# A gated recurrence and two gated feed-forward layers on one core: a step's loads one piece earlier in another order, its output gate a piece later, and one fold moved to where its result is read

## The chip, the cores and the metric

One core of a Trainium2 chip runs the whole program in one launch. The metric is the device time of that core in microseconds (us), lower is better. Three runs of the kernel before gave 875.76, 877.87 and 878.70 us, the median is 877.87 us.

## What is computed

The input is a recurrence over 768 time steps (4 sequences, 8 heads of 40 channels, the matrix state kept as `C`), and then two gated layers over the 3,072 tokens of 320 channels. Cut to what matters:

```python
for t in range(S):                                   # 768 steps
    m_new = np.maximum(f_gate[:, :, t] + m, i_gate[:, :, t])
    f_stab = np.exp(f_gate[:, :, t] + m - m_new)
    i_stab = np.exp(i_gate[:, :, t] - m_new)
    C = f_stab * C + i_stab * outer(vt, kt);  n = f_stab * n + i_stab * kt
    y[:, :, t] = sigmoid(o_gate[:, :, t]) * (C @ qt) / maximum(abs(n @ qt), 1)
x = (sigmoid(x @ w_gate) * (x @ w_val)) @ w_out      # d_ff 1536
h = x @ w_in;  out = (h * clip(h + 3, 0, 6) / 6) @ w_out   # d_ff 2048
```

## The kernel before, in words

The recurrence is done in 6 chunks of 128 time steps. One chunk of one sequence, (c, b), is called a step below, and is made in three pieces. Piece 0 (`att0`, L412) computes the scores on TensorE (L363), turns the decay rows of the step into a decay matrix by two scans on VectorE (L389), scales the values (L354, L383) and weighs the scores by the decays (L404). In the kernel before it also applies the sigmoid to the output gate, in place, on ScalarE (L410). Piece 1 (`att1`, L429) makes the outputs on TensorE: the part of the carried state (L445), the part inside the chunk (L456), and the state's increment (L471, not in the last chunk); then the denominators (L488 to L497), the product with the gate (L505) and the new state (L523, L526, L531). Piece 2 (`att2`, L533) transposes the result on TensorE (L537) and splits it into a rounded and a remaining part (L542 on ScalarE, L543 on VectorE). The pieces of a chunk run in the order 0.0, 0.1, 1.0, 0.2, 1.1, 2.0, 1.2, 2.1, 3.0, 2.2, 3.1, 3.2 (sequence.piece).

A step works on three tiles that are loaded from memory: `qk` (512 KB, L212), `vko` (values, keys, output gate; 480 KB, L215) and `dec` (the decay rows, one row read by all 128 partitions; 512 KB, L223). Each has two buffers, so the loads of step b + 2 go into the buffers of step b: `qk` is free after L445 of that step, `dec` after L456, and `vko` after L505.

The matrix multiplications of the first gated layer run between the pieces: in the main loop (L864) each pass over one block of 128 hidden channels takes at most two pieces, then the two products of the block (`m1_h`, L576; L555 to L562), then the output products of an earlier block (`m1_out`, L586; L597, L607), then, in every second pass from chunk 2 on, one job (`work`, L662) that fetches a block of raw second-layer weights (L94), converts it (L119, L122), combines it (L638 to L641) and stores it (L645, L646, L622). One of these stores, L646, writes runs of 128 bytes. Chunk c of the layer runs beside the recurrence of chunk c + 1, so in the last chunk of the layer there is none. At the end of a chunk `m1_end` (L609) copies the three accumulators out of PSUM. The third one holds two halves of 64 partitions that have to be added; the kernel before does that there: two half copies (L616, L617) and an addition (L618), then it stores the chunk to `x2_dram` (L619). The second layer (from L970) reads the chunks back in pairs (`x_load`, L793, at L801 and L803) and multiplies by a scheme of seven products (L914), with `m2_out` (L951 to L953) behind them.

PSUM has 8 banks: 3 for `mm`, 3 for `acc`, 2 for `att`. The scores of a step take both `att` banks until L404 has read them, its outputs take both until L491, its transposes one until L543.

All loads and stores are issued by one queue, that of SyncE (SP). Order is set in two ways. The text of the program gives the order within an engine among things that are ready, and a planner that knows only estimated durations may put an instruction ahead of earlier ones when it reckons its operands to be there; on the chip each engine then works through its queue in that fixed order, so that an instruction whose operand is late holds up all behind it. A block under `issue_after(ins)` puts its instructions behind `ins` on the engine of `ins`.

The head of the key product that reads past its own columns matters below: in L467 and L473 the columns of `vko` from the keys on are read in runs of 32, and the last run (head 7, second run) takes columns 312 to 343 of a 320-column key block, so it takes 24 columns of the output gate with it.

Of the kernel before, what the change touches and what calls it, by code (L numbers as in the profile page):

```python
# [8 lines left out]
F32 = mybir.dt.float32  # L9
# [11 lines left out]
NC = S // L  # L21
# [11 lines left out]
def mlstm_then_two_gated_ffn(  # L33
# [183 lines left out]
    def att_load(c, b):  # L217
        att_tiles(c, b)
        qk_load(c, b)
        vko_load(c, b)  # L220

    def dec_load(c, b):
        nc.sync.dma_start(  # L223
            out=at[c, b]["dec"].rearrange("p h l -> p (h l)"),
            in_=fz_dram[c, b * H : (b + 1) * H, :]
            .rearrange("h l -> (h l)")
            .rearrange("(o n) -> o n", o=1)
            .to_broadcast([P, H * L]),
        )
# [178 lines left out]
    def out_gate(c, b):  # L408
        o = at[c, b]["vko"][:, 2, :]
        nc.scalar.activation(out=o, in_=o, func=AF.Sigmoid)  # L410

    def att0(c, b, ps):  # L412
        scores(c, b, ps)
        if c == 1:
            values(c, b, True)
        value_ones(c, b)
        for n in range(2):
            decays(c, b, n)
        if c != 1:
            values(c, b, False)  # L420
        if c < NC - 1:
            values_end(c, b, c == 0)
        for n in range(2):
            weigh(c, b, n)

        with tc.issue_after(last_exp[-1]):
            out_gate(c, b)

    def att1(c, b, ps):  # L429

        outputs(c, b, ps)
        y = denominators(c, b)
        gated(c, b, y, c == 1 and b < 2)
        state(c, b)
# [141 lines left out]
    def m1_h(c, f, ts):  # L576
        n = ts.stop - ts.start
        banks = [ps_mm()[:, :n], ps_mm()[:, :n]]
        h_pair(slots["in", f], (1, c), banks, ts)
        g = gpool.tile([P, T], F32, tag="g", name="g")[:, :n]  # L580
        gate = nc.scalar.activation(out=g, in_=banks[0], func=AF.Sigmoid).ins  # L581
        nc.vector.tensor_tensor(out=g, in0=g, in1=banks[1], op=ALU.mult)  # L582
        gs[c, f, ts.start] = split_g(g)
        return gate
# [24 lines left out]
    def m1_end(c):  # L609
        a = acc1.pop(c)  # L610
        x2 = xpool.tile([P, 3, T], F32, tag="x2", name="x2")
        for m in range(2):
            nc.scalar.copy(out=x2[:, m, :], in_=a[m])

        sw = gpool.tile([P, T], F32, tag="g", name="sw")
        nc.scalar.copy(out=sw[0:64], in_=a[2][64:128])  # L616
        nc.scalar.copy(out=sw[64:128], in_=a[2][0:64])  # L617
        nc.vector.tensor_tensor(out=x2[:, 2, :], in0=sw, in1=a[2], op=ALU.add)  # L618
        nc.sync.dma_start(out=x2_dram[c], in_=x2)  # L619

    def store_w2(n, x):
# [171 lines left out]
    def x_load(pair):  # L793


        b = {}
        for k in range(2):
            for j in range(2):
                src = x2_dram[2 * pair + j]
                t = b[k, j] = late.tile([P, 640], F32, tag="c", name="xr", bufs=7)  # L800
                nc.sync.dma_start(out=t[:, 0:T], in_=src[:, k, :])  # L801
                for q in range(4):
                    nc.sync.dma_start(  # L803
                        out=t[32 * q : 32 * q + 32, T:],
                        in_=src[32 * k : 32 * k + 32, 2, q * P : (q + 1) * P],
                    )
        return x_combine(pair, b)

    def x_combine(pair, b):
# [54 lines left out]
    for i, (c, f, ts) in enumerate(steps):  # L864
        if i == halves[0] - 1:
            for b in range(2):
                att_load(1, b)
                dec_load(1, b)
        for _ in range(quota[i]):
            if pieces:  # L870
                cp, b, piece = pieces.pop(0)
                if cp > 0 and b == 0 and piece == 0:
                    x_tiles((1, cp))
                with ExitStack() as queued:
                    for ins in opened if cp == 0 else ():
                        queued.enter_context(tc.issue_after(ins))
                    (att0, att1, att2)[piece](cp, b, ps_att)
                nxt = divmod(cp * B + b + 2, B)
                if cp > 0 and piece == 2 and nxt[0] < NC:
                    att_load(*nxt)  # L880
                    dec_load(*nxt)
        gate = m1_h(c, f, ts)
        outputs_but(2 if i < n_two else 1)
        before.append((c, f, ts))
        if c == 0:
            work(1 if i < 2 * halves[0] else 2, n_w1)
        elif c < NC - 1:

            with tc.issue_after(gate):
                work(c > 1 and f % 2 == 0, n_jobs)  # L890
        elif f == 0:
            assert not jobs and not pieces
            early_sb.close()
            late = ctx.enter_context(tc.tile_pool(name="late", bufs=1, reuse_waits="tile"))
            x_parts = x_load(0)
            load_group(0)
        else:
            if f > 1 and f - 2 < F2 // 2:
                load_out2(f - 2)
            next(x_parts, None)  # L900
# [187 lines left out]
```

## Time and profile before

| what | value |
|---|---|
| median of three runs | 877.87 us |
| the profiled execution's own time | 880.01 us |
| its span, first to last instruction | 878.2 us |
| mean granted TensorE clock | 0.992 |
| TensorE matmul busy | 838.4 us (95%) |
| VectorE busy | 568.0 us (65%) |
| ScalarE busy | 399.3 us (45%) |
| share of the 16 DMA engines, queue of the loads and stores | 47.2% |

The span is 1.8 us shorter than the time of the same execution, which has its start and end around it. The profiled execution took 2.1 us more than the median. Granted clock means the share of full speed (2.4 GHz) that TensorE got. An engine that is idle costs time only when TensorE, which is busy nearly all the time, has to wait for it.

### The profile page before, as it was taken

What the parts mean: (1) busy time and instruction counts of PE and PEld (TensorE: products, weight loads), DVE (VectorE), ACT (ScalarE), POOL (GpSimd) and SP (SyncE); (2) the same over time, 40 slices, a digit from 0 to 9 for tenths busy, and PEclk for the clock granted to TensorE, in tenths of its full rate; (3) what the DMA queues carried; (4) which work ended last, traced back from release to release, by engine and by line L of the source; (5) the groups of instructions that cost most, each with busy time, mean ns of one, the idle gap of its engine ahead of it and who ended that gap; (6) DMA issues with size and microseconds to landing.
All of it is one profiled execution on the core that took longest, in us unless ns stands there. A gap on an engine that the chain in (4) does not pass through costs nothing.

```text
span 878.2 us, 17340 instructions
## 1 busy us (share of the span) xinstructions
PE 838.4 (95%) x7109; PEld 715.0 (81%) x7109; DVE 568.0 (65%) x1034; ACT 399.3 (45%) x813; POOL 2.5 (0%) x8
## 2 busy tenths in 40 slices
PE   6599899999999899989999999999999999999998
PEld 6488679887777777777778888888898888988898
DVE  7899965766587668655845553666746567466553
ACT  3687733332343234323322543556545555455542
POOL 1000000000000000000000000000000000000000
PEclk9999999999999999989999999999999999999999
DMA  9636723422655465456433632556734566344400
GB/s 356 224 116 214 253 72 108 143 72 72 200 202 177 156 200 203 156 176 198 142 85 94 178 85 73 181 163 185 235 99 147 153 197 220 109 151 146 146 31 31
DMA packets 67599, 134.86 MB, mean 154 GB/s; under 512 B 20672, under 2 KB 41600, under 8 KB 64448
## 3 DMA queue, kind: packets, MB, share of 16 engines
q1 hardware_dynamic: 67472, 133.65, 47.2%
q8 instruction: 56, 0.92, 0.5%
q14 instruction: 23, 0.19, 0.1%
q10 hardware_dynamic: 48, 0.10, 0.0%
HBM read 108.59 MB, written 25.13 MB: 152 GB/s over the span
## 4 chain that ended last, share of the span: by engine, by line
PE 80%; DVE 9%; DMA 8%; issue 2%; ACT 1%; SPq 0%; DVEq 0%; ACTq 0%
PE mm L914 9%; PE acc L597 9%; DMA dec<-fz_dram 7%; PE mm L561 6%; PE mm L560 6%; PE mm L559 6%; PE acc L914 4%; PE att L914 4%; PE mm L555 4%; PE mm L562 3%; PE acc L607 3%; DVE dec L389 3%; PE mm L951 2%; PE mm L953 2%; PE mm L952 2%; PE att L363 2%
## 5 line engine op out<-in xcount | busy, mean ns | idle before, releaser
L568 ACT CAST gh<-g 128x512 fp32r<-128x512 f32 (+1 forms) x130 | 76.1, 588 | 131.1 <-DVE g L582 109.0
L559 PE MATMUL mm<-x,w 128*128 128x512 f32 (+1 forms) x328 | 122.2, 373 | 0.0
L560 PE MATMUL mm<-x,w 128*128 128x512 f32 (+1 forms) x328 | 122.1, 372 | 0.0
L561 PE MATMUL mm<-x,w 128*128 128x512 f32 (+1 forms) x328 | 122.1, 372 | 0.0
L569 DVE TENSOR_TENSOR gl<-g,gh 128x512 fp32r<-128x512 f32 (+1 forms) x130 | 84.0, 648 | 55.9 <-ACT gh L568 55.1
L597 PE MATMUL acc<-gh,w 128*128 128x512 f32 (+1 forms) x328 | 104.2, 363 | 0.0
L914 PE MATMUL mm<-X,wg 128*128 128x512 f32 x336 | 85.5, 395 | 1.0 <-DMA wg<-wt_dram 1.0
L582 DVE TENSOR_TENSOR g<-g,mm 128x512 f32<-128x512 f32 (+1 forms) x82 | 50.6, 617 | 43.3 <-PE mm L562 43.2
L914 PEld LDWEIGHTS mm<-X,wg 128*128 128x128 f32 x336 | 61.9, 188 | 14.4 <-DMA wg<-wt_dram 1.2
L560 PEld LDWEIGHTS mm<-x,w 128*128 128x128 f32 x328 | 63.3, 193 | 11.1
L389 DVE TENSOR_TENSOR_SCAN dec<-dec,ident 128x512 f32<-128x512 f32 x40 | 48.0, 1217 | 37.5 <-DMA dec<-fz_dram 37.5
L561 PEld LDWEIGHTS mm<-x,w 128*128 128x128 f32 x328 | 63.1, 193 | 11.2
L559 PEld LDWEIGHTS mm<-x,w 128*128 128x128 f32 x328 | 63.6, 194 | 8.9
L555 PE MATMUL mm<-x,w 128*128 128x512 f32 (+1 forms) x164 | 68.0, 414 | 2.6 <-DVE cst L526 1.6
L581 ACT ACTIVATE g<-mm 128x512 f32<-128x512 f32 (+1 forms) x82 | 44.6, 544 | 54.3 <-PE mm L562 54.0
L597 PEld LDWEIGHTS acc<-gh,w 128*128 128x128 f32 x328 | 60.3, 188 | 10.5
L562 PE MATMUL mm<-x,w 128*128 128x512 f32 (+1 forms) x164 | 60.4, 368 | 0.0
L597 PE MATMUL acc<-gl,w 128*128 128x512 f32 (+1 forms) x164 | 59.9, 365 | 0.0
L929 ACT ACTIVATE gb<-c,half 128x512 f32<-128x512 f32 x48 | 34.3, 723 | 44.6 <-DVE c L925 44.5
L569 DVE TENSOR_TENSOR gl<-gb,gh 128x512 fp32r<-128x512 f32 x48 | 33.0, 691 | 30.6 <-ACT gh L568 30.6
L914 PE MATMUL att<-X,wg 128*128 128x512 f32 x168 | 46.9, 397 | 0.0
L568 ACT CAST gh<-gb 128x512 fp32r<-128x512 f32 x48 | 29.5, 620 | 37.1 <-PE att L952 37.1
(187 smaller groups left out, 1695.5 us busy)
## 6 DMA issues: line engine op xcount, KB each, us to landing
wg<-ws_dram SPq DMA_DIRECT2D x24, 1104.0 KB, 5.5
raw<-in_w SPq DMA_DIRECT2D x20, 640.0 KB, 4.0
qk<-in_qkT SPq DMA_DIRECT2D x22, 512.0 KB, 5.1
wg<-wt_dram SPq DMA_DIRECT2D x48, 224.0 KB, 6.3
vko<-in_vko SPq DMA_DIRECT2D x22, 480.0 KB
dec<-fz_dram SPq DMA_DIRECT2D x20, 512.0 KB, 5.0
raw<-in_wo SPq DMA_DIRECT2D x14, 640.0 KB, 3.8
X<-xt_dram SPq DMA_DIRECT2D x84, 64.0 KB, 3.1
```

The source lines that it names most:

```text
L389: nc.vector.tensor_tensor_scan(out=x, data0=a["factors"][n] if "factors" in a else x, data1=ident4.rearrange("p h l -> p (h l)"), initial= ...
L555: nc.tensor.matmul(out=banks[j], lhsT=tail, rhs=xl[:, 2, :], start=True, stop=False)
L559: nc.tensor.matmul(out=banks[j], lhsT=hi, rhs=xh[:, k, :], start=False, stop=False)
L560: nc.tensor.matmul(out=banks[j], lhsT=hi, rhs=xl[:, k, :], start=False, stop=False)
L561: nc.tensor.matmul(out=banks[j], lhsT=lo, rhs=xh[:, k, :], start=False, stop=False)
L562: nc.tensor.matmul(out=banks[j], lhsT=tail, rhs=xh[:, 2, :], start=False, stop=True)
L568: nc.scalar.copy(out=gh, in_=g)
L569: nc.vector.tensor_tensor(out=gl, in0=g, in1=gh.bitcast(F32), op=ALU.subtract)
L581: gate = nc.scalar.activation(out=g, in_=banks[0], func=AF.Sigmoid).ins
L582: nc.vector.tensor_tensor(out=g, in0=g, in1=banks[1], op=ALU.mult)
L597: nc.tensor.matmul(out=a[m], lhsT=lhsT, rhs=rhs, start=st and lhsT is hi and rhs is gh, stop=en and lhsT is lo, skip_group_check=True,)
L914: nc.tensor.matmul(out=ps, lhsT=w[a][s], rhs=x[:, b, :], start=first and i == 0, stop=i == 3, skip_group_check=True,)
```

## The change

There are three edits. The loads of the step after the next are written after piece 1 of a step, where they were written after piece 2, and in the order `dec`, `qk`, `vko` in place of `qk`, `vko`, `dec`. The sigmoid of the output gate is written in piece 1 behind the output matmuls, where it was at the end of piece 0. The two halves of the third accumulator are stored as they are, and are added when the second layer reads them: each of the four tail loads of a tile fetches both halves (32 KB, was 16 KB) into a new tile `xu`, and an addition of 128x128 elements on VectorE writes the tail. `xu` has the tag `xt`, whose three buffers the splits in `x_combine` use too.

```diff
+    def att1(c, b, ps):
+
+        outputs(c, b, ps)
         with tc.issue_after(last_exp[-1]):
             out_gate(c, b)
-
-    def att1(c, b, ps):
-
-        outputs(c, b, ps)
         y = denominators(c, b)
@@ def m1_end(c):
-        for m in range(2):
+        for m in range(3):
             nc.scalar.copy(out=x2[:, m, :], in_=a[m])
-
-        sw = gpool.tile([P, T], F32, tag="g", name="sw")
-        nc.scalar.copy(out=sw[0:64], in_=a[2][64:128])
-        nc.scalar.copy(out=sw[64:128], in_=a[2][0:64])
-        nc.vector.tensor_tensor(out=x2[:, 2, :], in0=sw, in1=a[2], op=ALU.add)
         nc.sync.dma_start(out=x2_dram[c], in_=x2)
@@ def x_load(pair):
                 nc.sync.dma_start(out=t[:, 0:T], in_=src[:, k, :])
+                u = late.tile([P, 2, P], F32, tag="xt", name="xu", bufs=3)
+                tails = src[:, 2, :].rearrange("(two k r) (q t) -> k q r two t", two=2, k=2, q=4)[k]
                 for q in range(4):
-                    nc.sync.dma_start(
-                        out=t[32 * q : 32 * q + 32, T:],
-                        in_=src[32 * k : 32 * k + 32, 2, q * P : (q + 1) * P],
-                    )
+                    nc.sync.dma_start(out=u[32 * q : 32 * q + 32], in_=tails[q])
+                nc.vector.tensor_tensor(out=t[:, T:], in0=u[:, 0], in1=u[:, 1], op=ALU.add)
@@ main loop
-                if cp > 0 and piece == 2 and nxt[0] < NC:
-                    att_load(*nxt)
+                if cp > 0 and piece == 1 and nxt[0] < NC:
+                    att_tiles(*nxt)
                     dec_load(*nxt)
+                    qk_load(*nxt)
+                    vko_load(*nxt)
```

## Rows read from the trace of the kernel before

**Rows 1.** Windows of core 0: stretch, then length and busy us of PE, PEld, DVE, ACT, POOL; clock, DMA.

```profile
100.00:460.00 360.00, 345.70 (x3766) 281.90 (x3766) 240.33 (x467) 125.73 (x272) 0.00 (x0) 0.98 0.46 150
...
540.00:878.00 338.00, 330.82 (x1840) 297.16 (x1838) 198.66 (x314) 178.74 (x308) 0.00 (x0) 1.00 0.47 147
```

**Rows 2.** Timeline of PE: start us, us, instruction, [idle before it <- releaser].

```profile
130.22 0.44 PE L537 MATMUL att<-ident,yo 128*128 128x128 f32 x2 [0.67 <-DVE dec L404]
...
244.11 0.38 PE L456 MATMUL att<-vi,dec 128*32 128x41 f32 x18 [1.97 <-DVE x L543]
...
300.01 0.38 PE L363 MATMUL att<-qk 40*128 40x128 f32 x2 [2.38 <-DVE x L543]
...
331.51 0.44 PE L456 MATMUL att<-vi,dec 128*32 128x41 f32 x16 [2.24 <-DVE x L543]
...
389.30 0.38 PE L363 MATMUL att<-qk 40*128 40x128 f32 x2 [2.45 <-DVE x L543]
...
421.56 0.32 PE L456 MATMUL att<-vi,dec 128*32 128x41 f32 x12 [1.50 <-DVE x L543]
```

**Rows 3.** Windows at a lower clock, columns as in Rows 1.

```profile
300.92:304.33 3.41, 3.41 (x11) 2.54 (x9) 2.46 (x4) 0.62 (x1) 0.00 (x0) 0.50 0.02 5
331.64:335.05 3.41, 3.41 (x100) 3.01 (x97) 2.55 (x8) 1.16 (x4) 0.00 (x0) 0.50 0.96 339
389.67:396.49 6.82, 6.82 (x27) 5.44 (x24) 2.76 (x5) 1.91 (x3) 0.00 (x0) 0.50 0.00 0
```

**Rows 4.** Waits between 100 and 460 us: engine, line, releaser: total us, times, longest us.

```profile
ACT vko L410 <- DMA vko<-in_vko: 56.3, 13, 6.7
DVE dec L389 <- DMA dec<-fz_dram: 37.5, 13, 5.7
...
DVE vi L354 <- DMA vko<-in_vko: 10.3, 3, 4.5
```

**Rows 5.** Timeline of DVE around 240 and 297 us, columns as in Rows 2.

```profile
238.08 2.34 DVE L389 TENSOR_TENSOR_SCAN dec<-dec,ident 128x512 f32<-128x512 f32 x2 [5.67 <-DMA dec<-fz_dram]
...
243.51 0.55 DVE L543 TENSOR_TENSOR x<-att,x 128x384 fp32r<-128x384 f32 x1
...
297.17 2.34 DVE L389 TENSOR_TENSOR_SCAN dec<-dec,ident 128x512 f32<-128x512 f32 x2 [4.20 <-DMA dec<-fz_dram]
```

**Rows 6.** Timeline of SP's queue: start us, us of the issue, line, transfer.

```profile
226.18 0.56 SPq L646 DMA_DIRECT2D wt_dram<-bits  x1
226.84 3.75 SPq L212 DMA_DIRECT2D qk<-in_qkT  x1
230.70 0.37 SPq L215 DMA_DIRECT2D vko<-in_vko  x1
231.12 0.42 SPq L223 DMA_DIRECT2D dec<-fz_dram  x1
...
288.37 3.15 SPq L212 DMA_DIRECT2D qk<-in_qkT  x1
291.62 0.38 SPq L223 DMA_DIRECT2D dec<-fz_dram  x1
```

**Rows 7.** Line L223: the landing of the decay rows after their issue.

```profile
DMA to landing us min/median/max: 4.9/5.0/5.6
```

**Rows 8.** Timeline of ACT around 298 us, columns as in Rows 2.

```profile
298.50 0.47 ACT L410 ACTIVATE vko<-vko 128x320 f32<-128x320 f32 x1 [6.26 <-DMA vko<-in_vko]
298.88 0.46 ACT L542 CAST x<-att 128x384 fp32r<-128x384 f32 x1
```

**Rows 9.** Lines L618, L819: duration ns min/median/max; then the landing of L803's loads.

```profile
L618 DVE TENSOR_TENSOR x<-sw,acc x6: 679/686/687, 140.0 to 548.8; 128x512 f32<-128x512 f32 x6
...
L819 DVE TENSOR_TENSOR xt<-xr,xt x21: 280/285/291, 473.7 to 754.7; 128x128 fp32r<-128x128 f32 x21
...
DMA to landing us min/median/max: 1.8/2.8/6.1
```

**Rows 10.** Timeline of PE at the end of a pair's first half.

```profile
623.48 0.41 PE L951 MATMUL acc<-w,gh 128*128 128x320 f32 x1 [1.33 <-ACT gh L568]
```

## The prediction, written before the change was run

> **What bounds the kernel now.** I first read the busy shares on the page and then the windows. TensorE is the bound: between 100 and 460 us, where the recurrence runs beside the first layer, it is busy for 345.70 of 360 us, so it idles for 14.3 us, and from 540 us on, in the second layer, it idles for 7.2 of 338 us [rows 1]. The stretch up to 460 us is the one that the moved loads touch. The timeline of PE then shows what ended its idle times there: six of them hold 11.2 of the 14.3 us, one ended by VectorE's weighing of scores (L404), five by its splitting of a transposed result (L543), which sets a bank of the two `att` banks free [rows 2]. So PE waits for VectorE, not for a load. Windows laid over the granted clock add a second price: after the gaps of 2.38, 2.24 and 2.45 us TensorE ran at 1.2 GHz in place of 2.4 for 3.41, 3.41 and 6.82 us; after those of 1.97 and 1.50 us it did not [rows 2, 3]. At half the clock half of these 13.6 us is lost, 6.8 us. All that this stretch can give back is therefore 14.3 + 6.8 = 21.1 us, 2.4%.
>
> Next I read why VectorE is late. The view of the waits names two transfers: the scans waited 37.5 us for `dec`, 13 times; ScalarE's sigmoid waited 56.3 us for `vko`, 13 times, and the values another 10.3 us for it [rows 4]. The scan at 238.08 us sits in VectorE's queue 5.67 us before its rows are there, and L543 at 243.51 us, for which PE waits, stands behind it [rows 5]. In the same way the sigmoid holds up ScalarE: at 298.50 us it had waited 6.26 us, and the first half of the split (L542), without which L543 can't start, came right behind it [rows 8].
>
> Last, SP's queue shows why `dec` is late: the transfer that follows a store of short runs (L646) takes 3.75 us to issue, `vko` comes next, and `dec` is issued at 231.12 us and usable at 238.08, 6.96 us later, where decay rows with less ahead of them need 5.0 [rows 5, 6, 7].
>
> **The change part by part.** *Order and place of the loads.* Each of the three issues stays, with its bytes; none is added. SP already takes the loads as soon as the buffers are free, ahead of text that comes earlier: they stand right behind L646, which belongs to a job of an earlier pass and keeps its place before them [rows 6]. So I cost the earlier place by itself at nothing, with bounds of 0 and, where a fetch or store is passed, one issue of 0.4 us [rows 6], 16 times, 6.4 us at most. `vko` keeps its wait for L505 and holds up on SP what is behind it, a fetch or a chunk's store, as it does now; `dec` has to wait for L456 a little after L445, and `qk` behind it that much longer, but `qk` is wanted a full step later. The order is worth more. At 226.84 us `dec` would take the slow place: its issue ends at 230.59 and began at 230.2 at the latest, it lands 5.0 us later at 235.2, 2.9 us earlier than 238.08 [rows 5, 6, 7]. At 288.37 us only `qk` stood before it: the issue would count from 291.1, landing at 296.1 for 297.17, 1.1 us earlier [rows 5, 6, 7].
>
> The rule that I weigh against this row is that of the Trainium skill, page "DMA: Bandwidth & Descriptors", section "Anatomy of one DMA — SWDGE (gpsimd) path": about 2.0 us fixed and the bytes at 436 GB/s, an estimate of 3.2 us for 512 KB, fitted on another queue path than SP's. The trace has 5.0 us, never under 4.9 [rows 7], and decides; by the page every load would land 1.8 us sooner still, the gaps at 300.01 and 331.51 us would close, and the sum below would be 2.9 us more, 867.4 us.
>
> Gap by gap [rows 2]: 244.11, 1.97 us, closes, since 2.9 us is more than that: 1.97. 300.01: two scans of 2.34 us behind 296.1 end at 298.4, L543 comes at 298.4 for 299.4 if ScalarE is out of the way (next part): 1.0, which leaves 1.4. 331.51: there the values wait for `vko` too, which now comes last, so I take 0.7, which leaves 1.5. 421.56: the same in the last chunk, 0.3. 389.30: nothing, see below. 130.22: `dec` was issued when it could be, only `qk` goes out of its way, 0.5 of 0.67. The rest of the idle time, 3.1 us in pieces under these, 0.3. Sum 4.8 us, bounds 0 (if the scans move up as much as the rows do) and 14.3. The clock: 1.4 and 1.5 us are nearest to the gaps after which it stayed, so two stretches of 3.41 us go, 2 x 1.7 = 3.4 us; bounds 0 and 6.8 [rows 3].
>
> *The sigmoid.* By text it only moves; but the increment (L471) reads 24 columns of the gate with the keys, so behind it the sigmoid has to wait for L471 where before L471 waited for the sigmoid. That takes it off the landing of `vko` and puts it in the 3 us or so in which VectorE makes the denominators; 0.47 us [rows 8] on ScalarE is covered by them, and if they did not cover it, it would cost 0.47 per step. In the last chunk there is no L471: nothing ties the sigmoid, it may stay at the landing of `vko`, and so I leave 389.30 and its 6.82 us at half clock as they are [rows 2, 3]. Its worth is in the 1.0 and 0.7 above.
>
> *The fold.* Six times ScalarE is rid of a copy and VectorE of 0.69 us [rows 9]; none of PE's large idle times is ended there [rows 2], so nothing, bounds 0 and 0.69 each. In its place come 12 additions of 128x128, 4 before each pair; the nearest row is L819 with 0.285 us [rows 9]. The first four run in the long last chunk of the first layer. The others stand in the second layer, where VectorE is busy 59% [rows 1]; at the end of a pair's first half PE waits 1.33 us for a chain through VectorE and ScalarE [rows 10], and I let one addition fall into it: 0.3, twice, 0.6 us. Bounds: nothing, and a full landing before it, below.
>
> Sum: 4.8 + 3.4 - 0.6 = 7.6 us. The profiled execution took 880.01 us and would take 872.4; it was 2.1 us over the median of 877.87, so for the median I say **870.3 us**.
>
> **The rivals.** *All gaps close.* If rows land before the planner's place for the scans everywhere, 21.1 - 0.6 = 20.5 us go: 857.4 us. For it speaks that one reason is named for 104 us of waits [rows 4]; against it that near 130 us and 389 us the load has nothing to pass.
>
> *The scans move along.* The planner placed the scans where it reckoned the rows to be there. If it reckons them earlier, it puts scans and values further up, VectorE stands still just as long, and L543 stays behind it; the gain is 0 and the fold's 0.6 us remains: 878.5 us, no change. The place of the scan at 238.08, far ahead of its use, speaks for it [rows 5]; against it, that the delay at SP comes from a slow issue of 3.75 us [rows 6], of which a planner with estimated durations need not know.
>
> *The additions stall the second layer.* They are queued on VectorE and wait for a load that lands after 2.8 us, in one case 6.1 [rows 9]. If one landing stands ahead of the chain that PE waits for, the gap of 1.33 us [rows 10] grows by 2.8 + 0.3 = 3.1 us, which brings it to more than all gaps after which the clock fell, and 1.7 to 3.4 us are lost with that [rows 2, 3]: 4.8 to 6.5 us in each of two pairs, 9.6 to 13.0, in the middle 11.3. Against the 8.2 us gained before the fold this is 3.1 us slower, 881.0 us. It decides from 4.1 us a pair on. Against it: VectorE idles 41% there [rows 1], and the loads come a group ahead of that gap.
>
> **How the numbers follow.** The forecast has a chance of 0.48, its own range is 864 to 876. All gaps close 0.14, scans move along 0.20, additions stall 0.18. A measurement of this kernel can tell 0.3% from no change, that is 2.6 us, from 875.2 to 880.5. Forecast and closing together give 0.62 faster, the moving scans 0.20 the same, the stall 0.18 slower. The range reaches from 857.4 to the middle of the stall, 881.0; outside are half of the stall and the outer edges.
>
> **What would show it.** Right: scans around 238 and 297 us wait under 3.5 and 3.2 us, L410 waits for L471 in chunks 2 to 4 and for `vko` in the last alone, windows around 300 and 331 us at full clock, PE idles about 9.5 us between 100 and 460 us. Wrong: `dec` still issued behind another load after L646; the waits at L389 still near 37 us; gaps at L951 over 2 us; new idle times between 540 us and the end.

## The result and the profile after

The changed kernel took 881.91 us (median of 11 runs, 877.32 to 885.85), the kernel before 877.16 us beside it (11 runs): the ratio is 1.0052, 95% interval 1.0027 to 1.0077. One of those 11 runs took 921.19 us, 5% more than the rest, and is not in the ratio. The changed kernel is half a per cent slower, where faster was forecast. The profiled execution of the changed kernel (884.24 us) has a span of 882.4 us at a mean granted clock of 0.986; the one before (880.01 us) had 878.2 us and 0.992. Each took some 2 to 3 us more than its median, so the two can be compared.

The page after, its first lines and the engines' shares of the chain that ended last:

```profile
span 882.4 us, 17342 instructions
...
PE 842.0 (95%) x7109; PEld 719.2 (82%) x7109; DVE 568.2 (64%) x1040; ACT 397.7 (45%) x807; POOL 2.5 (0%) x8
...
PE 78%; DVE 12%; DMA 7%; issue 2%; ACT 1%; SPq 0%; DVEq 0%; ACTq 0%
```

The same shares before:

```profile
PE 80%; DVE 9%; DMA 8%; issue 2%; ACT 1%; SPq 0%; DVEq 0%; ACTq 0%
```

VectorE has 568.2 us of work, as before (568.0), but its share of the chain rose from 9% to 12%, and the transfers' 7% (8% before) are nearly all `dec` (7% in both). So VectorE does no more work and yet stands in the way more often.

Windows of the changed kernel, columns as in [rows 1]:

```profile
100.00:460.00 360.00, 342.75 (x3733) 280.60 (x3734) 235.43 (x459) 122.27 (x263) 0.00 (x0) 0.97 0.46 151
...
540.00:878.00 338.00, 336.50 (x1865) 301.69 (x1864) 201.88 (x322) 179.83 (x309) 0.00 (x0) 1.00 0.47 146
```

In the first stretch TensorE idles for 360 - 342.75 = 17.3 us, where it idled for 14.3 [rows 1], and its clock fell to 0.97. In the second it idles for 1.5 us, where it idled for 7.2 (the stretches are not quite the same work, since the changed kernel comes to them later). Measured by marks in the program, the recurrence up to the last transpose (L537 before, L536 after) ends at 474.8 us in place of 467.7, 7.1 us later; from there to the second layer's first product it is 72.0 us in both; the second layer takes 335.6 us in place of 338.5, 2.9 us less. 7.1 - 2.9 is the 4.2 us of the two spans.

Idle times of PE in the changed kernel (columns as in [rows 2]; those of 2.94, 1.49 and 0.99 us at 100.94, 168.19 and 181.37 us are left out):

```profile
150.68 0.38 PE L363 MATMUL att<-qk 40*128 40x128 f32 x2 [1.85 <-DVE x L542]
...
243.31 0.69 PE L536 MATMUL att<-ident,yo 128*128 128x128 f32 x2 [2.37 <-DVE dec L404]
...
307.44 0.49 PE L363 MATMUL att<-qk 40*128 40x128 f32 x4 [2.77 <-DVE x L542]
...
338.74 0.43 PE L455 MATMUL att<-vi,dec 128*32 128x41 f32 x12 [1.99 <-DVE x L542]
...
394.91 0.49 PE L363 MATMUL att<-qk 40*128 40x128 f32 x4 [1.25 <-DVE x L542]
...
427.20 0.43 PE L455 MATMUL att<-vi,dec 128*32 128x41 f32 x20 [3.50 <-DVE x L542]
```

Line numbers from the output matmuls on are one lower than before (L542 is L543, L455 is L456). The last four gaps stand before the same instructions as those at 300.01, 331.51, 389.30 and 421.56 us in [rows 2]; 2.38, 2.24, 2.45 and 1.50 us before, they are 2.77, 1.99, 1.25 and 3.50. The gap of 1.97 us at 244.11 is gone; in its step PE now waits 2.37 us a little earlier, before a transpose (L536), for the weighing (L404). The gap at 150.68 us is new.

The stretches at half clock (columns as in [rows 1], the clock is the first 0.50):

```profile
150.95:157.78 6.83, 6.83 (x38) 6.48 (x36) 2.86 (x7) 0.79 (x2) 0.00 (x0) 0.50 0.01 2
243.11:246.53 3.42, 3.22 (x9) 2.68 (x10) 3.35 (x7) 0.00 (x0) 0.00 (x0) 0.50 0.33 137
307.97:311.38 3.41, 3.41 (x16) 2.70 (x13) 2.73 (x5) 0.62 (x1) 0.00 (x0) 0.50 0.00 0
338.69:342.10 3.41, 3.37 (x100) 2.99 (x101) 2.58 (x7) 1.47 (x4) 0.00 (x0) 0.50 1.02 332
396.71:400.13 3.42, 3.42 (x10) 2.65 (x9) 1.72 (x3) 0.83 (x2) 0.00 (x0) 0.50 0.00 0
427.43:430.85 3.42, 3.42 (x68) 2.85 (x56) 2.50 (x8) 0.82 (x2) 0.00 (x0) 0.50 0.98 306
```

Together 23.9 us against 13.6 [rows 3]; at half the clock half of it is lost, so this is 5.1 us more. With 3.0 us more idle time it is an estimate of some 8 us, near the 7.1 us by which the recurrence ends later.

Why VectorE is late is in the waits between 100 and 460 us (columns as in [rows 4]), in SP's queue and in VectorE's timeline around 240 us and 304 us:

```profile
DVE dec L389 <- DMA dec<-fz_dram: 53.9, 15, 8.8
...
ACT vko L410 <- DMA vko<-in_vko: 18.8, 4, 8.2
```

```profile
231.78 0.56 SPq L640 DMA_DIRECT2D wt_dram<-bits  x1
232.44 3.78 SPq L223 DMA_DIRECT2D dec<-fz_dram  x1
236.26 0.43 SPq L212 DMA_DIRECT2D qk<-in_qkT  x1
...
295.56 3.44 SPq L212 DMA_DIRECT2D qk<-in_qkT  x1
299.09 0.38 SPq L223 DMA_DIRECT2D dec<-fz_dram  x1
```

```profile
240.33 2.34 DVE L389 TENSOR_TENSOR_SCAN dec<-dec,ident 128x512 f32<-128x512 f32 x2 [5.47 <-DMA dec<-fz_dram]
242.59 1.26 DVE L404 TENSOR_TENSOR dec<-att,dec 128x512 f32<-128x512 f32 x2
...
247.94 0.55 DVE L542 TENSOR_TENSOR x<-att,x 128x384 fp32r<-128x384 f32 x1
...
304.60 2.34 DVE L389 TENSOR_TENSOR_SCAN dec<-dec,ident 128x512 f32<-128x512 f32 x2 [4.57 <-DMA dec<-fz_dram]
306.86 0.53 DVE L542 TENSOR_TENSOR x<-att,x 128x384 fp32r<-128x384 f32 x1
```

VectorE before, at the same weighing:

```profile
231.13 1.28 DVE L404 TENSOR_TENSOR dec<-att,dec 128x512 f32<-128x512 f32 x2
```

The sigmoid's wait for `vko` went from 56.3 us to 18.8, and `dec` is indeed the first load behind the store at 231.78 us. The scan begins 240.33 - 232.34 = 8.0 us after the issue of that store ended (231.78 + 0.56); before it was 238.08 - 226.74 = 11.3 us [rows 5, 6]. The rows are there 3.3 us earlier, and still the scan waits 5.47 us, where it waited 5.67 [rows 5]: it was moved up in VectorE's queue as far as its rows came forward. What is more, it now stands ahead of the weighing L404. Before, the weighing had run at 231.13 us and the scan came after it; now the weighing, for which PE waits at 243.31 us, sits behind the scan for rows that belong to another step.

In the order of VectorE's compiled queue, which the trace repeats, this can be seen without times. Y is the product with the gate (L505), W a weighing, S a scan, v the values, g the gate's split (L569), X the split of the result (L543), at the step around 240 us:

```
before                       Y g W W S S v g X g
changed kernel               Y g S S W W v g X g
```

At others the scans move ahead of the values or of the weighing too ("W W v S S" becomes "W W S S v", "g v g X S S" becomes "g S g S X v"). That the planner reckons the rows earlier is the likely reason; the runs show the order that it made, not what it reckoned.

### The profile page after: what moved, and what is told of

The parts are those of the page before. It is cut to its first block, busy times and chain, and to the rows that moved or that the text cites. A ratio compares the mean times of both kernels' runs of the same rounds, so it can differ in the third digit from the quotient of the medians.

```text
span 882.4 us, 17342 instructions
## 1 busy us (share of the span) xinstructions
PE 842.0 (95%) x7109; PEld 719.2 (82%) x7109; DVE 568.2 (64%) x1040; ACT 397.7 (45%) x807; POOL 2.5 (0%) x8
## 4 chain that ended last, share of the span: by engine, by line
PE 78%; DVE 12%; DMA 7%; issue 2%; ACT 1%; SPq 0%; DVEq 0%; ACTq 0%
PE mm L910 9%; PE acc L596 8%; DMA dec<-fz_dram 7%; PE mm L558 6%; PE mm L559 6%; PE mm L560 6%; PE att L910 5%; PE acc L910 4%; PE mm L554 4%; DVE dec L389 3%; PE mm L561 3%; PE acc L606 3%; PE mm L947 2%; PE acc L947 2%; PE mm L948 2%; PE mm L949 2%
## 5 line engine op out<-in xcount | busy, mean ns | idle before, releaser
L568 DVE TENSOR_TENSOR gl<-g,gh 128x512 fp32r<-128x512 f32 (+1 forms) x130 | 84.2, 647 | 57.2 <-ACT gh L567 56.8
L389 DVE TENSOR_TENSOR_SCAN dec<-dec,ident 128x512 f32<-128x512 f32 x40 | 48.0, 1216 | 53.9 <-DMA dec<-fz_dram 53.9
L559 PEld LDWEIGHTS mm<-x,w 128*128 128x128 f32 x328 | 64.3, 196 | 11.2
L560 PEld LDWEIGHTS mm<-x,w 128*128 128x128 f32 x328 | 64.2, 196 | 11.3
L558 PEld LDWEIGHTS mm<-x,w 128*128 128x128 f32 x328 | 64.5, 197 | 9.0
L568 DVE TENSOR_TENSOR gl<-gb,gh 128x512 fp32r<-128x512 f32 x48 | 33.1, 690 | 32.3 <-ACT gh L567 32.3
```

The costliest lines, as they stand in the source:

```text
L389: nc.vector.tensor_tensor_scan(out=x, data0=a["factors"][n] if "factors" in a else x, data1=ident4.rearrange("p h l -> p (h l)"), initial= ...
L558: nc.tensor.matmul(out=banks[j], lhsT=hi, rhs=xh[:, k, :], start=False, stop=False)
L559: nc.tensor.matmul(out=banks[j], lhsT=hi, rhs=xl[:, k, :], start=False, stop=False)
L560: nc.tensor.matmul(out=banks[j], lhsT=lo, rhs=xh[:, k, :], start=False, stop=False)
L568: nc.vector.tensor_tensor(out=gl, in0=g, in1=gh.bitcast(F32), op=ALU.subtract)
```

## The experiments

The theory was: the order of the loads makes the planner reckon the decay rows earlier, it puts the scans further up in VectorE's queue, and there they block what PE waits for. The rivals were that the sigmoid or the later additions cost the time, or that the loads' earlier place on SP does. Ratios are against the kernel before on the same chip, with 95% intervals.

**Each edit alone.** First the loads only.

```diff
-                if cp > 0 and piece == 2 and nxt[0] < NC:
-                    att_load(*nxt)
+                if cp > 0 and piece == 1 and nxt[0] < NC:
+                    att_tiles(*nxt)
                     dec_load(*nxt)
+                    qk_load(*nxt)
+                    vko_load(*nxt)
```

> The kernel before with the edit of the loads alone. Theory A (the planner moves the scans up with the rows, and the stretch of VectorE behind a scan that waits holds up the split or the weighing that sets an att bank free): this edit alone carries the loss, 881 to 884 us, PE idle of about 18 us between 100 and 460 us and at least four stretches at half clock there, the waits at L389 over 45 us. Rival B (the sigmoid, now behind the increment, is what delays): this edit alone is no slower than before, 874 to 878 us. Rival C (the transfers themselves are slower or later, whatever the order on VectorE): 881 to 884 us too, with the scans standing where they stood before.

881.68 us, 1.0043 (1.0017 to 1.0070): the loads alone make nearly the whole loss. PE idles for 16.1 us between 100 and 460 us, a little less than expected, five stretches are at half clock, and the waits at L389 are 49.7 us. In the traces of this kernel and of the one before, SP takes the same transfers in the same order but for `dec`, which is ahead of one or two others at six places; PE's order differs at two places and VectorE's at five, all of them in the recurrence. The sigmoid only:

```diff
     def att1(c, b, ps):
         outputs(c, b, ps)
+        with tc.issue_after(last_exp[-1]):
+            out_gate(c, b)
```

> The kernel before with the sigmoid's edit alone. Theory A: 875 to 878 us, ScalarE waits under 25 us for vko in place of 56 us, and PE's idle time between 100 and 460 us stays within 2 us of the 14.3 us of before. Rival B: 880 to 884 us, with PE's gaps ended by the product with the gate or by what stands behind the sigmoid on ScalarE. Rival C: as A.

878.23 us, 1.0009 (0.9992 to 1.0027). Its wait for `vko` fell here too, to 17.3 us in four waits, and it bought nothing. The fold only, both its halves:

```diff
-        nc.vector.tensor_tensor(out=x2[:, 2, :], in0=sw, in1=a[2], op=ALU.add)
...
+                nc.vector.tensor_tensor(out=t[:, T:], in0=u[:, 0], in1=u[:, 1], op=ALU.add)
```

> The kernel before with the fold's edit alone. Theory A: 873 to 876 us, since the profile of the changed kernel has 1.4 us of idle time before L947 and L910 from 540 us on where before had 4.1 us; no new wait of VectorE for the tail loads. Rival D (the additions stall the second layer): over 879 us, gaps over 2 us behind 600 us.

872.89 us, 0.9954 (0.9930 to 0.9977): the part that the prediction priced as a small cost is a gain of some 4 us, a little more than expected here.

**Order or place.** The new order at the old place:

```diff
                 if cp > 0 and piece == 2 and nxt[0] < NC:
-                    att_load(*nxt)
+                    att_tiles(*nxt)
                     dec_load(*nxt)
+                    qk_load(*nxt)
+                    vko_load(*nxt)
```

> The kernel before with the decay rows first, at the old place (after piece 2). On VectorE this puts the scans exactly where the edit of the loads puts them. Theory A (the order, by moving the scans in VectorE's queue, is the whole loss): as slow as the edit of the loads, 880 to 883 us, waits at L389 of 45 to 52 us. Rival E (the earlier place is the loss, by the order in which SP takes the transfers): 875 to 878 us.

882.04 us, 1.0063 (1.0039 to 1.0086). The old order at the new place:

```diff
-                if cp > 0 and piece == 2 and nxt[0] < NC:
+                if cp > 0 and piece == 1 and nxt[0] < NC:
```

> The kernel before with the loads one piece earlier, in the old order. VectorE's queue is that of before, and SP's differs in two fetches and three stores. Theory A: no change, 876 to 879 us, waits at L389 of 35 to 40 us. Rival E: 880 to 883 us.

878.13 us, 1.0001 (0.9982 to 1.0021). The order is the cost, the place is nothing. VectorE's compiled queue says the same: with the new order alone it is that of the loads edit, with the new place alone it is that of before. The other two edits without the loads, against the changed kernel:

```diff
-                if cp > 0 and piece == 1 and nxt[0] < NC:
-                    att_tiles(*nxt)
-                    dec_load(*nxt)
-                    qk_load(*nxt)
-                    vko_load(*nxt)
+                if cp > 0 and piece == 2 and nxt[0] < NC:
+                    att_load(*nxt)
+                    dec_load(*nxt)
```

> The changed kernel with the loads as they were before: the sigmoid's and the fold's edits together. Theory A: the fold's gain stays, 872 to 875 us, 0.9945 to 0.9975 of before. If the two edits spoil each other without the loads' edit (rival F: the loss of the whole change is not in the loads alone), 877 us or more.

874.71 us, 0.9964 (0.9943 to 0.9985), the product of the two alone (1.0009 x 0.9954 = 0.9963).

**Holding the scans back.** If the place of the scans is what costs, then pinning them behind the last split written before them must turn the loss into a gain. In the changed kernel:

```diff
+    last_lo = []
...
-        for n in range(2):
-            decays(c, b, n)
+        with ExitStack() as behind:
+            if c > 0:
+                behind.enter_context(tc.issue_after(last_lo[-1]))
+            for n in range(2):
+                decays(c, b, n)
...
+        last_lo.append(lo.ins)
         return hi.ins, lo.ins
```

> The changed kernel with one line more: the scans of a step are issued behind the split (the second instruction of piece 2) that was written last, on VectorE, by an order without a semaphore. Theory A: the waits at L389 fall under 10 us, PE's idle time between 100 and 460 us under 6 us, no more than one stretch at half clock, 862 to 869 us. Rival C: the rows are late for the weighing too, L404 or the scan still holds PE, 876 us or more.

871.38 us, 0.9943 (0.9921 to 0.9965). The sigmoid's and the fold's edits without the loads gave 0.9964, so with the scans pinned nothing is left of the loads' loss; but the 862 to 869 us expected were not reached. The waits between 100 and 460 us tell why:

```profile
DVE vi L355 <- DMA vko<-in_vko: 48.4, 12, 10.0
```

The values now stand ahead of the splits and wait for `vko`, the last load in the new order, where they waited 10.3 us in three waits before [rows 4]. The place at the head of the queue was taken by the next instruction that waits for a load. So I tied the values as well:

```diff
             for n in range(2):
                 decays(c, b, n)
-        if c != 1:
-            values(c, b, False)
+            if c != 1:
+                values(c, b, False)
```

> As the kernel with the tied scans, with the values (L354 in piece 0) tied behind the same split. In the run before the values, now ahead of the split, waited 48 us for vko and ended in gaps of 4.91 and 3.17 us. Theory A (any instruction of a later step that waits for a load ahead of the split costs the same): both gaps under 1 us, at most one stretch at half clock between 100 and 460 us, 860 to 867 us. Rival C (the loads are late for their use as well): a new wait for vko or dec at the weighing or at vd, 870 us or more.

861.41 us, 0.9821 (0.9792 to 0.9849). TensorE idles for 5.2 of the 360 us; the gap of 4.91 us is gone, but one of 2.32 us is left at 405.73 us, with a stretch at half clock:

```profile
100.00:460.00 360.00, 354.76 (x3919) 290.99 (x3920) 247.82 (x480) 129.46 (x274) 0.00 (x0) 0.99 0.46 151
...
ACT vko L411 <- DMA vko<-in_vko: 18.6, 4, 8.9
DVE x L546 <- ACT x L545: 8.1, 6, 5.5
```

The same ties with the loads as they were before:

```diff
-                if cp > 0 and piece == 1 and nxt[0] < NC:
-                    att_tiles(*nxt)
+                if cp > 0 and piece == 2 and nxt[0] < NC:
+                    att_load(*nxt)
                     dec_load(*nxt)
-                    qk_load(*nxt)
-                    vko_load(*nxt)
```

> The kernel with scans and values tied behind the split, but its loads as before: after piece 2, qk, vko, dec. Theory A (the loads were early enough for their use in either order; only the place in VectorE's queue cost): the same within 2 us, 860 to 864 us. Rival G (with the queue mended, rows that land 1 to 3 us earlier do pay): 865 us or more, with waits of the scans for dec behind the split.

862.79 us, 0.9826 (0.9807 to 0.9845). Once no scan or value can block the queue, the order of the loads matters no more: the ratios 0.9821 and 0.9826 lie within each other's intervals. In the traces PE and VectorE have the same order in both kernels.

**The last chunk's sigmoid.** The four waits for `vko` that were left on ScalarE belong to the last chunk, and the first half of the split (here L545) is held up by them; in the last chunk I put the sigmoid behind that split:

```diff
-        with tc.issue_after(last_exp[-1]):
+        with tc.issue_after(last_hi[-1] if c == NC - 1 else last_exp[-1]):
             out_gate(c, b)
...
+        last_hi.append(hi.ins)
```

> As the kernel with scans and values tied, and in the last chunk the sigmoid is issued behind the first instruction of the split that was written last, on ScalarE. In the run before, PE's largest idle time between 100 and 460 us was 2.32 us at 403 us, behind a split whose first half stood behind a sigmoid that waited for vko, and a stretch at half clock followed. Theory A: that gap and that stretch go, 3 to 4 us, 857 to 859.5 us, ScalarE's waits for vko under 8 us. If the gap has another cause: 861 us and the gap stays.

857.72 us, 0.9764 (0.9745 to 0.9783): the best version of this study, faster than both kernels, before by 2.4%. The chain by engine, the window up to 449 us (the recurrence ends earlier), its wait at the scans, and VectorE around the same step:

```profile
PE 87%; DVE 8%; ACT 2%; issue 1%; DMA 0%; DVEq 0%; ACTq 0%
...
100.00:449.00 349.00, 346.53 (x3893) 284.92 (x3894) 245.18 (x475) 128.75 (x271) 0.00 (x0) 1.00 0.47 155
...
DVE dec L391 <- DMA dec<-fz_dram: 2.6, 2, 1.8
...
230.15 1.29 DVE L406 TENSOR_TENSOR dec<-att,dec 128x512 f32<-128x512 f32 x2 [0.40 <-PE att L365]
...
236.82 0.55 DVE L547 TENSOR_TENSOR x<-att,x 128x384 fp32r<-128x384 f32 x1
237.29 2.33 DVE L391 TENSOR_TENSOR_SCAN dec<-dec,ident 128x512 f32<-128x512 f32 x2
```

The transfers' share of the chain is 0%, where the changed kernel had 7%. The weighing runs when its scores are there, the split before the scan, and the scan begins without a wait. PE idles for 2.5 us in 349.

**The ties without the change.** Scans and values pinned in the kernel before, none of the three edits:

```diff
-        for n in range(2):
-            decays(c, b, n)
-        if c != 1:
-            values(c, b, False)
+        with ExitStack() as behind:
+            if c > 0:
+                behind.enter_context(tc.issue_after(last_lo[-1]))
+            for n in range(2):
+                decays(c, b, n)
+            if c != 1:
+                values(c, b, False)
```

> The kernel before with scans and values tied behind the split and none of the three edits. Theory A (place in VectorE's queue is the lever, and the sigmoid's waits for vko are the next one): waits at L389 under 5 us, but ScalarE still waits for vko in front of the first half of the split, so 865 to 872 us. If VectorE's queue alone decides: 862 to 865 us (the fold's 2 to 4 us short of the kernel with all edits).

875.86 us, 0.9990 (0.9971 to 1.0008): no difference, where 865 to 872 us were expected. The scans' wait is gone, but ScalarE's is not. Its wait between 100 and 460 us, then ScalarE's timeline and PE's behind it:

```profile
ACT vko L411 <- DMA vko<-in_vko: 58.9, 16, 6.8
...
415.26 0.47 ACT L411 ACTIVATE vko<-vko 128x320 f32<-128x320 f32 x1 [6.51 <-DMA vko<-in_vko]
415.63 0.58 ACT L586 ACTIVATE g<-mm 128x512 f32<-128x512 f32 x1
...
416.26 0.50 PE L560 MATMUL mm<-x,w 128*128 128x512 f32 x1 [2.56 <-ACT g L586]
```

With the sigmoid at its old place it waits 6.51 us for `vko`; the layer's own gate (L586) stands behind it and holds a bank of `mm`, for which PE waits 2.56 us. Three more of the long gaps of this run have the same head: at 160.39, 330.22 and 390.17 us PE waits 2.33, 1.41 and 1.15 us for chains that begin behind a sigmoid that had waited 2.79, 5.63 and 6.25 us. So two queues had each a waiting instruction at their head. The ties alone give 0.9990, the sigmoid and the fold without ties 0.9964, the three together (with the loads as before) 0.9826: 1.3% less than the product of 0.9954. This is not the fold's doing: in the profiled executions the recurrence ends at 468.5 us with the ties alone (an execution 3.8 us over its median) and at 452.7 with all three, while the second layer, where the fold's gain lies (below), differs by 1.8 us (337.4 and 335.6).

**The two halves of the fold.** Only what it does at the chunk's end, with the addition left out altogether:

```diff
-        for m in range(2):
+        for m in range(3):
             nc.scalar.copy(out=x2[:, m, :], in_=a[m])
-        sw = gpool.tile([P, T], F32, tag="g", name="sw")
...
-        nc.vector.tensor_tensor(out=x2[:, 2, :], in0=sw, in1=a[2], op=ALU.add)
```

> The kernel before with the fold taken out of the chunk's end and not made at all: the tail loads fetch the first half of the accumulator alone, the other half is left out. Theory H (the gain of the fold is the chunk's end: three copies in place of four and an addition, accumulator banks free earlier): 872 to 874.5 us, as the fold's edit, with PE's idle time behind 600 us as before (1.33 us twice). Theory I (the gain comes from the late additions, which shift the combining of the next pair behind the chain at the end of a pair's first half): 875.5 to 878 us.

877.11 us, 0.9990 (0.9970 to 1.0009). Only the late additions, the old fold kept, so that the tails come out twice as large:

```diff
...
+                    nc.sync.dma_start(out=u[32 * q : 32 * q + 32], in_=tails[q])
+                nc.vector.tensor_tensor(out=t[:, T:], in0=u[:, 0], in1=u[:, 1], op=ALU.add)
```

> The kernel before, fold at the chunk's end kept, with the doubled tail loads and the late additions on top: the tails are added to themselves, so they come out twice as large. Theory H: 876.5 to 879 us, not faster. Theory I: 872 to 875 us, with the idle times of 1.33 us behind 600 us down to 0.5 us.

873.22 us, 0.9950 (0.9931 to 0.9969): both times are those of Theory I, though not for its reason. The gain comes from what looks like a cost: 12 more instructions, and 16 KB more in each tail load. The end of a pair's first half shows how. Lines of PE, ScalarE and VectorE before, behind which comes the gap of 1.33 us in [rows 10]:

```profile
620.17 1.09 PE L914 MATMUL mm<-X,wg 128*128 128x512 f32 x4
621.83 0.31 PE L953 MATMUL att<-w,gl 128*128 128x320 f32 x1
...
621.36 0.69 ACT L929 ACTIVATE g<-mm,half 128x512 f32<-128x512 f32 x1 [0.60 <-PE mm L914]
...
620.52 0.82 DVE L834 TENSOR_TENSOR xr<-xr 128x640 f32<-128x640 f32 x1
622.08 0.69 DVE L930 SCALAR_TENSOR_TENSOR g<-g,mm 128x512 f32<-128x512 f32 x1
```

and with the late additions:

```profile
616.10 1.09 PE L914 MATMUL mm<-X,wg 128*128 128x512 f32 x4
618.63 0.31 PE L953 MATMUL att<-w,gl 128*128 128x320 f32 x1
619.39 0.41 PE L951 MATMUL acc<-w,gh 128*128 128x320 f32 x1 [0.45 <-ACT gh L568]
...
615.36 0.81 DVE L834 TENSOR_TENSOR xr<-xr 128x640 f32<-128x640 f32 x1
618.00 0.69 DVE L930 SCALAR_TENSOR_TENSOR g<-g,mm 128x512 f32<-128x512 f32 x1 [0.62 <-ACT g L929]
```

From the end of the last product (L914) the chain through L929, L930 and L568 to L951 takes the same 2.2 us in both: 623.48 - 621.26 and 619.39 - 617.19. What differs is PE's order. Before, six output products (L951 to L953) stand behind the last product and end at 622.14; with the additions twelve stand there and end at 618.94, so PE has 0.9 us more to do while the chain runs, and the gap is 0.45 us in place of 1.33. The same holds at the end of the next pair's first half (0.46 us in place of 1.33). The combination of the next pair (L834) also moved up on VectorE, but PE did not wait for it before: the product at 622.08 begins as soon as L929 ends (621.36 + 0.69). So the fold, too, acts by the order that the planner makes; why the additions change it no run shows. The second layer takes 335.1 to 335.6 us in every profiled execution with the late additions and 337.3 to 338.7 in every one without, 335.3 and 335.1 with the fold and with its late half against 338.5 before. The two gaps make 1.8 us of this; the rest was not followed gap by gap.

**What is left.** The parts multiply to 1.0043 x 1.0009 x 0.9954 = 1.0006, while the whole is 1.0052. Two pairs of the edits, as diffs against the changed kernel. The loads with the fold (the sigmoid taken back to `att0`):

```diff
     def att0(c, b, ps):
...
+        with tc.issue_after(last_exp[-1]):
+            out_gate(c, b)
     def att1(c, b, ps):
         outputs(c, b, ps)
-        with tc.issue_after(last_exp[-1]):
-            out_gate(c, b)
```

> The changed kernel with the sigmoid back in piece 0: the loads' and the fold's edits together. VectorE's queue in the recurrence is that of the loads' edit. Theory J (the whole change is slower than its parts' product, 1.0007, because the sigmoid's edit costs where the scans are early): the parts' product, 876 to 879.5 us. Theory K (the fold's gain is lost beside the loads' edit): 880.5 us or more.

877.83 us, 1.0004 (0.9980 to 1.0028), against a product of 0.9997: beside the loads the fold keeps its worth.

The loads with the sigmoid (the fold taken back to the chunk's end):

```diff
-                nc.vector.tensor_tensor(out=t[:, T:], in0=u[:, 0], in1=u[:, 1], op=ALU.add)
...
+        nc.vector.tensor_tensor(out=x2[:, 2, :], in0=sw, in1=a[2], op=ALU.add)
```

> The kernel before with the loads' and the sigmoid's edits together. Theory J: slower than the loads' edit alone, 883.5 to 888 us, with more stretches at half clock. Theory K: as the loads' edit alone, 880 to 883 us.

882.21 us, 1.0054 (1.0034 to 1.0074), against a product of 1.0052: beside the loads the sigmoid costs what it does alone. Neither pair holds the missing 0.5%; it shows only with all three together and is not much wider than the intervals. In the profiled executions the second layer of the whole change keeps the fold's gain (335.6 us), so what is missing lies in the recurrence, which ends at 474.8 us with all three edits and at 470.5 with the loads and the sigmoid, although the scans stand at the same places of VectorE's queue in both. Half clock does not settle it: between 100 and 460 us it is 23.9 us in the whole change and 20.5 with the loads and the sigmoid, and the 6.8 us with the loads and the fold come from an execution of 872.85 us, the fastest of that kernel and 5 us under its median. Where the missing part comes from stays open.

## Why the prediction was wrong

The forecast was 870.3 us, the measured median is 881.91. The recurrence was to give back 8.2 us and ends 7.1 us later; the second layer was to cost 0.6 us and takes 2.9 us less.

**What bounds the kernel: right.** PE waited for VectorE, and VectorE for `dec`. With that wait and ScalarE's out of the way 2.4% was to be had, near the 21.1 us that the prediction counted: the best version took 878.38 - 857.72 = 20.7 us less than the kernel before beside it, 3 to 4 of these from the fold. That it comes out at the 857.4 us of the rival "all gaps close" is in part luck, since the fold stands in that price with the wrong sign. One reading of the rows was off without weight: the "pieces under these" hold a gap of 1.29 us at 163.30 us, ended by the weighing, more than the 0.67 us that was counted.

**The loads, their place: right.** Priced at nothing, measured 1.0001.

**The loads, their order: the transfers right in one step of two, the gain wrong.** The row at 226.84 us was to land 2.9 us earlier; counted from the store it was 3.3. The one at 288.37 us was to land 1.1 us earlier and did not: on SP `qk` still stood first there, it took the slow issue of 3.44 us, `dec` followed at 299.09, and the scan began 9.0 us after that slow issue did (304.60 - 295.56), where it had been 8.8 (297.17 - 288.37) [rows 5, 6]. The rule of the Trainium skill, page "DMA: Bandwidth & Descriptors", section "Anatomy of one DMA — SWDGE (gpsimd) path", by which 512 KB would take an estimated 3.2 us, did not hold on SP's queue here: `dec` takes 5.1 us to its landing in the changed kernel, where it took 5.0 [rows 7].

**Gap by gap: the step that failed.** "244.11, 1.97 us, closes, since 2.9 us is more than that" holds only if L404 stays ahead of the scan and the scan stays where it was ahead of L543. The step took VectorE's order from the trace of before and moved only the times in it. But that order is made by the planner, and the loads' order alone changes it, as the run with the new order at the old place shows (1.0063). The lower bound of 0, "if the scans move up as much as the rows do", was taken without a reason that excludes a loss; there was none. In place of a gain of 4.8 us the idle time grew by 3.0, and the weighing, for which the prediction had counted only the 0.67 us at 130.22, ended a gap of 2.37 us. The clock's term had the same fault: 3.4 us were to come back, and 5.1 went, since gaps that were to shrink or go were still there and three more were followed by half clock (150.68, 243.31, 427.20).

**The rival "the scans move along": right mechanism, wrong price.** It was given 0.20 and a gain of 0, "VectorE stands still just as long". It does, 5.47 us for 5.67; but the price of a wait is what stands behind it, and the scans passed the weighing on their way up. With the loads alone the time is 0.4% longer, and with the scans pinned this is gone. No rival of the prediction ended slower in this way.

**The sigmoid: right, for a reason that was half seen.** It waits for L470 of the changed kernel (L471 of before), 0.6 us in all, and for `vko` only in the last chunk; this cost nothing. Alone it gave nothing, and the 1.0 and 0.7 us in which the prediction saw its worth were not among what was gained. That it has to move before the gain behind VectorE's queue can be had, 0.9990 with the old place against 0.9826 with the new one and the fold, was not in the sum.

**The fold: the term mis-sized.** -0.6 us was put down as a cost, for additions that fall into the chain at the end of a pair's half; it measured a gain of 0.46%, 4 us. The additions did not fall into the chain; with them PE's order puts six more output products behind the last product, while the chain takes the same 2.2 us. That it is a gain is luck: nothing in the edit aimed at it. The rival "the additions stall the second layer" is out: the gap at L951 shrank to 0.45 us.

**The signs named.** The waits of the scans under 3.5 and 3.2 us were 5.47 and 4.57; the windows around 300 and 331 us were at half clock still; PE idled 17.3 us and not 9.5. Each said "wrong", as did `dec` issued behind another load at 299.09 us and the waits at L389, 53.9 us where "still near 37" was named. Of the signs for "right" only the sigmoid's waits came; gaps at L951 over 2 us and new idle times behind 540 us did not appear.

## What to carry to other kernels

Where a planner sets each engine's order, an edit of the loads is an edit of the consumers' places too: a load that comes sooner can pull its consumer up, and the price is what the consumer then stands in front of, not how long it waits. So compare the order of the instructions on the engines before the times, and pin the instruction that waits for a load behind the one that the busiest engine waits for. Look for such a head-of-queue wait on each engine of the chain: here, mending VectorE's alone (0.9990) or ScalarE's alone (1.0009) gave nothing, and both together, with the fold's 0.5%, gave 1.7%.

## What the runs showed of the hardware

The length of a gap alone does not tell what it does to TensorE's clock. It stayed at 2.4 GHz after gaps of 1.97 and 1.50 us in the kernel before, and in the changed kernel it was at 1.2 GHz for 3.41 us from the end of a gap of 1.99 us (338.74) on, in the 3.42 us that begin soon after a gap of 1.25 us (394.91) and in the 6.83 us after one of 1.85 us (150.68). One gap has the same length and the same releaser in two kernels. PE in the changed kernel:

```profile
100.94 0.50 PE L554 MATMUL mm<-x,w 128*128 128x512 f32 x1 [2.94 <-DVE cst L525]
```

and in the best version, with a window behind it (columns as in [rows 1]):

```profile
101.75 0.50 PE L561 MATMUL mm<-x,w 128*128 128x512 f32 x1 [2.94 <-DVE cst L530]
...
103.07:106.48 3.41, 3.41 (x10) 2.65 (x9) 3.41 (x6) 2.89 (x12) 0.00 (x0) 0.50 0.51 185
```

In the changed kernel the clock stayed at 2.4 GHz behind this gap (1.00 from 101.00 to 104.40 us), and in the best version it was at 1.2 GHz for 3.41 us. The prediction's step "nearest to the gaps after which it stayed" is not safe therefore: a forecast has to keep the clock's bounds open for gaps of this size.

The slow issue on SP belongs to the place and not to the transfer: behind the store of short runs it was `qk` with 3.75 us [rows 6] and in the changed kernel `dec` with 3.78, while the `qk` after that took 0.43. It gets less with time: in the kernel before, the 13 transfers that SP began within 0.6 us of the end of such a store's issue took 3.0 to 4.0 us, and those begun 1.5, 1.8 and 2.1 us after it took 2.2, 1.6 and 1.2.
